# One attention and channel-mix kernel: early constants, diagonals in pieces, and another order of transposes, loads and gate products

## The chip, the cores and the metric

The kernel runs on one core of one Trainium2 chip. The metric is the device time of an execution in microseconds (us). TensorE (PE) multiplies matrices; VectorE (DVE), ScalarE (ACT) and GpSimd (POOL) work elementwise; SyncE (SP) issues DMA transfers, which 16 DMA engines carry out. Each engine runs its own instructions strictly in order, and an instruction waits at the head of its engine's queue until what it needs is there.

## The reference

Two layers, in float32. The first is a local attention over 768 positions in 24 chunks of 32: a chunk's queries see 16 keys to the left, its own 32, 8 to the right, and 8 memory keys. The second is a channel mix on the attention's output x, `[4, 768, 512]`:

```
xk = mu_k * x + (1.0 - mu_k) * x_prev        # x_prev: x one position earlier
xr = mu_r * x + (1.0 - mu_r) * x_prev
k  = np.maximum(xk @ w_k, 0.0)               # 512 -> 1024
v  = k * k @ w_v                             # 1024 -> 512
r  = 1.0 / (1.0 + np.exp(-(xr @ w_r)))       # 512 -> 512
out = r * v
```

The weights arrive as 64-bit floats, and the kernel turns each 1 MB chunk of them into two float32 parts, high and low. Every product of the channel mix is made of three matmuls (high x high, high x low, low x high).

## The kernel before, in words

The 3072 positions are worked on in 12 units of 256, each of two tiles of 128. An operation has a name of a kind and a number. For unit u: `s` scores, `max`, `sub`, `exp`, `sum`, `norm` the softmax. For tile t: `qk`, `vw` the loads of its queries and keys, and of its values; `t` the transposes of the softmax (tile pt), `bd` the two copies of these out of PSUM into `aTz`, `a` the products with the values (tile px), `x` their copy. Then, for unit u again, `mix` (for unit 0 done on PE with diagonal matrices, tile xf; for units 1 and 2 on DVE from a difference `df`), `xh`, `xl` the high and low parts of the mixed input, `g` the gate products (pr, in the last units gps and gpc), `h` the hidden products (ph), `relu`, `sq`, `kh`, `kl`, `v` the value products (pv), `sig` the sigmoid, `o` and `out`. The ten weight chunks are `w0` to `w9` (w0, w1 of w_r; w2 to w5 of w_k; w6 to w9 of w_v): `load`, `mag` on ACT, `low` and `join` on DVE, then `hi` and `lo`. Block `h0.n` of unit 0 needs chunk w(2+n), `g0.n` chunk wn, `v0.n` chunk w(6+n).

From unit 3 on the value products, from unit 6 on the hidden products, and in the last two units the gate products are made with seven block products in place of eight. The weight forms that this needs lie in DRAM and are loaded per unit (`f`, tiles wkh, wkl, wvh, wvl from `forms`).

Two things set the order on every engine. The list `FIRST` (L52) names operations one after the other, with the engine of each; they are recorded in just that order. What it doesn't name, a planner (`Plan.walk`) places by estimated costs and due times, and the due times come from the order of PE's products, `te_order`, whose lead is `LEAD` and which places the last units by rules. So a change in `FIRST` or in `te_order` also moves operations on ACT, DVE and POOL behind it, and can give an operation with a choice to another engine. Buffers of one kind (`big` for qk loads and raw weights, `vw`, `m` for PSUM banks) are handed on in turn, so a load waits on SP for the last reader of its buffer, and all loads behind it wait too.

Around the change: L393 and L394 issue the identity and mu from SP. `diagonals(m)` records for each m one operation `dg{m}` on ACT with nine instructions: (1 - mu), then four diagonals of mu and four of (1 - mu), which `mix0.m` reads. L1815 to L1819 hold back the later qk and vw loads: such a load waits for the first product whose due time lies 3 behind that of a given `a` or `s`. L1828 fills PE's idle time at the start with matmuls on zeros (tile warm) as long as no hidden product of unit 0 has been recorded.

Of the kernel before, what the change touches and what calls it, by code (L numbers as in the profile page):

```python
# [51 lines left out]
FIRST = """  # L52
qk0@dma s0@pe qk1@dma max0@dve sub0@dve exp0@act s0b@pe max0b@dve mu@dma id@dma sum0@dve norm0@pool qk3@dma qk2@dma
w2.load@dma dg1@act vw0@dma vw1@dma w3.load@dma sub0b@dve exp0b@act sum0b@dve norm0b@dve dg0@act w2.mag@act s1@pe
t0@pe w4.load@dma bd0.0@act t1@pe w2.low@dve bd0.1@dve a0@pe w2.join@dve w2.hi@dve max1@dve sub1@dve qk5@dma
w2.lo@pool bd1.0@act bd1.1@act a1@pe qk4@dma x0@act x1@act mix0.0@pe mix0.1@pe w3.low@dve w3.mag@act w3.join@dve
vw2@dma exp1@act vw3@dma sum1@dve w5.load@dma w4.low@dve norm1@dve w4.mag@act w4.join@dve xh0.0@act w3.hi@act t2@pe
xl0.0@dve s2@pe xh0.1@act w4.hi@act bd2.0@act w0.load@dma bd2.1@dve w1.load@dma t3@pe bd3.1@act bd3.0@act a2@pe x2@act
xl0.1@dve w3.lo@dve qk6@dma a3@pe max2@dve h0.0@pe w4.lo@pool w5.mag@act w5.low@dve x3@act sub2@dve w5.join@dve
h0.1@pe h0.2@pe w0.low@dve vw4@dma exp2@act w0.mag@act sum2@dve w1.low@dve w5.hi@act w5.lo@dve h0.3@pe qk7@dma  # L60
w1.mag@act w0.join@dve w0.hi@act norm2@dve t4@pe w1.join@dve t5@pe w0.lo@dve relu0.1@act df1@dve relu0.0@act sq0.0@act
vw5@dma w1.hi@act bd5.1@act bd4.0@act w1.lo@dve sq0.1@act s3@pe g0.0@pe g0.1@pe relu0.2@act w7.load@dma mix1.1@dve
w6.load@dma mix1.0@dve bd4.1@act sq0.2@act kh0.1@act bd5.0@act xh1.1@dve xl1.1@dve w7.low@dve kl0.1@dve kh0.2@act
w8.load@dma xh1.0@act a4@pe xl1.0@dve kh0.0@act relu0.3@act kl0.0@dve w8.low@dve w7.mag@act w6.mag@act w9.load@dma
w7.join@dve w6.low@dve w6.join@dve sig0.0@act sig0.1@act a5@pe g1.0@pe g1.1@pe h1.0@pe sq0.3@act kh0.3@act h1.1@pe
kl0.3@pool x4@dve w7.hi@act x5@dve max3@dve sub3@dve sig1.0@act w7.lo@pool kl0.2@dve relu1.0@act sig1.1@act w6.hi@act
df2@dve w8.mag@act sq1.0@act w9.low@dve w6.lo@dve h1.2@pe h1.3@pe relu1.2@act relu1.1@act w9.mag@act relu1.3@act
sq1.2@act v0.0@pe w8.join@dve w9.join@dve sq1.3@act w8.hi@act mix2.1@dve v0.1@pe exp3@act w9.hi@act w8.lo@dve v0.2@pe
kh1.0@dve kl1.0@dve sq1.1@act w9.lo@dve kh1.1@act kl1.1@dve xh2.1@act xl2.1@dve mix2.0@dve kh1.2@act kl1.2@pool
v0.3@pe  # L70
"""
# [228 lines left out]
def local_attention__then__channel_mix(  # L300
# [1523 lines left out]
    busy = 0.0  # L1824
    with tc.manual_schedule():
        for o in plan.order(FIRST.split()):
            if o.eng == "pe":
                n = 0 if ("ph", 0, 0) in T else int((o.start - busy - 0.1) / (0.86 if busy else 1.72))  # L1828
                for _ in range(n):
                    warm = warm or ps("mat0", "warm")  # L1830
                    nc.tensor.matmul(warm, zero, zeros, start=True, stop=True)
# [51 lines left out]
```

## Time and profile before

| | us |
|---|---|
| median of 3 runs | 390.83 (390.39 to 391.03) |
| profiled execution | 391.06 |
| its span, first to last instruction | 389.3 |

| engine | busy us | share of the span |
|---|---|---|
| PE | 380.3 | 98% |
| DVE | 336.6 | 86% |
| ACT | 274.2 | 70% |
| POOL | 16.0 | 4% |

Times in the trace count from the start of the span. The profiled execution is 1.76 us longer than its span. A busy PE is not a useful PE: the matmuls on zeros count as busy, and matmuls overlap, so that the time between two starts says more than the duration of one.

### The profile page before, as it was taken

Reading aid. Unit: us, or ns where it says so; the run is one execution under the profiler, and the core shown is the slowest. Engines: PE = TensorE matmul, PEld = TensorE weight load, DVE = VectorE, ACT = ScalarE, POOL = GpSimd, SP = SyncE. Lnnn points to the kernel's source line nnn. Section 1 sums busy time; section 2 is a strip of 40 time slices with the busy share of each in tenths; the row PEclk is TensorE's granted clock in tenths of the full one; section 3 lists DMA queues with packets and bytes.
Section 4 is the critical chain, followed back from the end, with each engine's and each line's share of the span. In section 5 each row is a group of like instructions: output and inputs, shape, how many; then the busy total and the mean of one; then the engine's idle time right before and its main releaser. Section 6 shows DMA issues by size and latency. Waiting matters only on the chain.

```text
span 389.3 us, 11106 instructions
## 1 busy us (share of the span) xinstructions
PE 380.3 (98%) x4768; PEld 352.4 (91%) x4768; DVE 336.6 (86%) x570; ACT 274.2 (70%) x468; POOL 16.0 (4%) x15
## 2 busy tenths in 40 slices
PE   7799999999999999999999999999999999999996
PEld 3589889888988999999999999999999899999996
DVE  3699999888898999969989989898999797978784
ACT  3877796914796789676578689877587857588741
POOL 2221004010000000000010000000000000000000
PEclk9999999999999999999999999999999999999999
DMA  8999870411053345435387576644056611043011
GB/s 313 414 374 368 318 309 2 141 56 54 2 197 124 130 137 199 148 127 223 117 298 226 190 272 206 209 182 145 2 163 183 199 53 56 28 136 109 0 56 54
DMA packets 25344, 63.43 MB, mean 163 GB/s; under 512 B 2512, under 2 KB 9040, under 8 KB 24784
## 3 DMA queue, kind: packets, MB, share of 16 engines
q1 hardware_dynamic: 25296, 62.73, 45.5%
q8 instruction: 37, 0.61, 0.6%
q14 instruction: 11, 0.09, 0.1%
HBM read 52.24 MB, written 10.49 MB: 161 GB/s over the span
## 4 chain that ended last, share of the span: by engine, by line
PE 91%; DMA 5%; ACT 2%; DVE 1%; SPq 0%; issue 0%
PE ph L1374 15%; PE pr L1350 14%; PE pc L1710 10%; PE pv L1350 9%; PE pa L1710 6%; PE B L1069 6%; PE pb L1710 6%; PE px L619 6%; PE G L1069 4%; PE A L1069 4%; PE s L522 4%; PE pt L602 2%; DMA vw<-in_vw_dram 2%; PE xf L673 2%; DMA wvl<-forms 1%; PE gps L1274 1%
## 5 line engine op out<-in xcount | busy, mean ns | idle before, releaser
L1374 PE MATMUL ph<-xh,wkh 128*128 128x256 f32 x192 | 53.5, 279 | 0.0
L1374 PE MATMUL ph<-xh,wkl 128*128 128x256 f32 x192 | 53.2, 277 | 0.1
L1374 PE MATMUL ph<-xl,wkh 128*128 128x256 f32 x192 | 53.1, 276 | 0.0
L1374 PEld LDWEIGHTS ph<-xh,wkl 128*128 128x128 f32 x192 | 36.1, 188 | 0.3 <-DVE wkl L450 0.3
L1374 PEld LDWEIGHTS ph<-xh,wkh 128*128 128x128 f32 x192 | 36.0, 188 | 0.3
L1374 PEld LDWEIGHTS ph<-xl,wkh 128*128 128x128 f32 x192 | 36.1, 188 | 0.0
L1657 DVE TENSOR_TENSOR khl<-k,khl 128x512 fp32r<-128x512 f32 x42 | 28.8, 688 | 6.2 <-ACT khl L377 5.7
L1350 PE MATMUL pr<-wrh,xh 128*128 128x512 f32 x80 | 31.4, 392 | 0.0
L1350 PE MATMUL pr<-wrh,xl 128*128 128x512 f32 (+1 forms) x97 | 31.3, 351 | 0.0
L1350 PE MATMUL pr<-wrl,xh 128*128 128x512 f32 x80 | 31.2, 390 | 0.0
L377 ACT CAST khl<-k 128x512 fp32r<-128x512 f32 x47 | 29.2, 621 | 2.2 <-PE pa L1710 0.9
L1350 PE MATMUL pv<-wvh,khl 128*128 128x512 f32 (+1 forms) x97 | 30.3, 390 | 0.0
L1710 PE MATMUL pa<-wvh,khl 128*128 128x256 f32 x144 | 28.2, 281 | 0.0
L1710 PE MATMUL pc<-wtbig,khl 128*128 128x256 f32 x216 | 28.2, 280 | 0.0
L377 ACT COPY aTz<-pt 64x512 f32<-64x512 f32 x43 | 24.8, 580 | 4.0 <-PE pt L602 3.6
L1710 PE MATMUL pb<-wtx,khl 128*128 128x256 f32 x216 | 27.6, 277 | 0.0
L1477 ACT ACTIVATE k<-ph 128x512 f32<-128x512 f32 x23 | 13.5, 597 | 19.1 <-PE ph L1374 17.1
L619 PEld LDWEIGHTS px<-aTz,vw 128*64 128x64 f32 x768 | 23.5, 138 | 3.5 <-DVE aTz L379 1.7
L1710 PEld LDWEIGHTS pc<-wtbig,khl 128*128 128x128 f32 x216 | 26.0, 188 | 0.1
L619 PE MATMUL px<-aTz,vw 128*64 128x64 f32 x768 | 25.5, 224 | 0.6 <-DVE aTz L379 0.6
L1710 PEld LDWEIGHTS pb<-wtx,khl 128*128 128x128 f32 x216 | 26.0, 188 | 0.0
L1710 PEld LDWEIGHTS pa<-wvh,khl 128*128 128x128 f32 x144 | 23.1, 188 | 0.3
(215 smaller groups left out, 1042.8 us busy)
## 6 DMA issues: line engine op xcount, KB each, us to landing
vw<-in_vw_dram SPq DMA_DIRECT2D x24, 512.0 KB, 5.1
ring<-in_qk_dram SPq DMA_DIRECT2D x16, 672.0 KB, 5.8
out_dram<-o SPq DMA_DIRECT2D x22, 256.0 KB, 2.1
qk<-in_qk_dram SPq DMA_DIRECT2D x8, 672.0 KB, 6.3
raw<-in_w_k_dram SPq DMA_DIRECT2D x4, 1024.0 KB, 7.5
raw<-in_w_v_dram SPq DMA_DIRECT2D x4, 1024.0 KB, 7.7
wvh<-forms SPq DMA_DIRECT2D x12, 256.0 KB, 3.4
wvl<-forms SPq DMA_DIRECT2D x12, 256.0 KB, 3.8
```

The costliest lines, as they stand in the source:

```text
L377: e.copy(dst, src)
L522: nc.tensor.matmul(room(h, c)[CHUNK * j : CHUNK * (j + 1), r, :], q4[z, r, j, :], k3[z, r, STEP * j : STEP * j + NK], start=True, stop=True,)
L602: nc.tensor.transpose(p[:, n * P : (n + 1) * P], e[:, n // 2, c, n % 2, :], id_sb)
L619: nc.tensor.matmul(p3[64 * h : 64 * h + 64, 2 * g : 2 * g + 2, CHUNK * j : CHUNK * j + CHUNK], v[:, g, h, j, :], a[:, h, g, j, :], start=True,
L673: nc.tensor.matmul(z, T["diag", m][:, j, k], x[:, k, 1 - j : 1 - j + UTOK], start=j == 0, stop=j == 1)
L1069: nc.tensor.matmul(z, w, x[:, k], start=q in (1, 7) and i + k + m == 0, stop=i + k == 2 and m == 2, skip_group_check=q not in (1, 7),)
L1274: nc.tensor.matmul(z, xs[x][:, k, c * P : (c + 1) * P], ws[w][:, k], start=q in (1, 7) and c + k + m == 0, stop=c + k == 2 and m == 2, ski ...
L1350: nc.tensor.matmul(p[:, a : a + step], x, w[:, a : a + step], start=start, stop=stop and a + step == DM)
L1374: nc.tensor.matmul(z, w, x[:, k], start=start, stop=stop)
L1477: e.activation(r, T["ph", u, f], AF.Relu)
L1657: nc.vector.tensor_sub(T["al", u, name], block(at), T["ah", u, name].bitcast(F32))
L1710: nc.tensor.matmul(p, l[:, i], r[i], start=start, stop=stop, skip_group_check=not fresh)
```

## The change

Four edits. The identity and mu are loaded from ACT's queue, as the first entries of `FIRST`. `diagonals` records three operations for each m: `mu{m}`, `dg{m}a` (four diagonals of mu), `dg{m}b` (four of 1 - mu), and `FIRST` places them apart. `FIRST` is a new list, longer than before (it now reaches into unit 2); in it, among much else, `t0` stands ahead of `s1`, `t2`, `t3`, `s2` and `a2` follow each other, `a3` and `s3` stand behind unit 0's hidden products, and the vw3 load behind qk7. In `te_order` two gate products of the last pair of units stand earlier, and the value load of tile 22 (`2 * NU - 2`) is held back to a due time 9 behind instead of 3.

```diff
 FIRST = """
-qk0@dma s0@pe qk1@dma max0@dve sub0@dve exp0@act s0b@pe max0b@dve mu@dma id@dma sum0@dve norm0@pool qk3@dma qk2@dma
+id@dma mu@dma qk0@dma mu1@act s0@pe qk1@dma mu0@act max0@dve sub0@dve dg1a@act s0b@pe dg1b@act max0b@dve sub0b@dve
+exp0@act sum0@dve qk3@dma qk2@dma norm0@dve dg0a@act t0@pe s1@pe exp0b@act sum0b@dve w2.load@dma norm0b@dve vw0@dma
...
@@ te_order
                 if u == nu - 2:
                     r = [("g", u, n) for n in range(len(GATES))]
-                    seq += h[:12] + r[:2] + v[:2] + h[12:] + r[2:5] + v[2:]
+                    seq += h[:12] + r[:2] + v[:2] + h[12:] + r[2:5] + v[2:5] + r[5:6] + v[5:]
...
             elif u == nu - 1:
-                seq += r[5:6] + v[:2] + r[6:] + v[2:]
+                seq += r[6:] + v
@@ the body of the kernel
-    o_id = op("id", ("dma", 0.2), lambda: nc.sync.dma_start(id_sb, ident))
-    o_mu = op("mu", ("dma", 0.1), lambda: nc.sync.dma_start(mu_sb[:, 0:2], mu))
+    o_id = op("id", ("dma", 0.2), lambda: nc.scalar.dma_start(id_sb, ident))
+    o_mu = op("mu", ("dma", 0.1), lambda: nc.scalar.dma_start(mu_sb[:, 0:2], mu))
@@ diagonals(m)
-        def f():
+        def f_rest():
+            nc.scalar.activation(mu_sb[:, 2 + m], mu_sb[:, m], AF.Copy, scale=-1.0, bias=1.0)
+
+        def f(j):
             T["diag", m] = k2[m].rearrange("p i t -> p (i t)").rearrange("p (j k n) -> p j k n", j=2, k=KT)
-            nc.scalar.activation(mu_sb[:, 2 + m], mu_sb[:, m], AF.Copy, scale=-1.0, bias=1.0)
-            for j in range(2):
-                for k in range(KT):
-                    nc.scalar.activation(T["diag", m][:, j, k], id_sb, AF.Copy, scale=mu_sb[:, m + 2 * j, k : k + 1])
+            for k in range(KT):
+                nc.scalar.activation(T["diag", m][:, j, k], id_sb, AF.Copy, scale=mu_sb[:, m + 2 * j, k : k + 1])
 
-        diag[m] = (op(f"dg{m}", ("act", 2.0), f, [o_id, o_mu], new=d), d)
+        o = op(f"mu{m}", ("act", 0.2), f_rest, [o_mu])
+        o = op(f"dg{m}a", ("act", 1.22), lambda: f(0), [o_id, o], new=d)
+        diag[m] = (op(f"dg{m}b", ("act", 1.22), lambda: f(1), [o], use=d), d)
@@ the late loads
-            o.deps.append(next(y for y in line if y.due > x.due + 3))
+            o.deps.append(next(y for y in line if y.due > x.due + (9 if o.name == f"vw{2 * NU - 2}" else 3)))
@@ the matmuls on zeros
-                n = 0 if ("ph", 0, 0) in T else int((o.start - busy - 0.1) / (0.86 if busy else 1.72))
+                n = 0 if ("xf", 0, 0, 0) in T or ("xf", 0, 1, 0) in T else int((o.start - busy - 0.1) / (0.86 if busy else 1.72))
```

ACT before, from its first instruction: `e` is the softmax of unit 0 in two halves (L550), `k_81` and `k_80` hold the diagonals of m = 1 and m = 0 (L407), `xx` the magnitude of w2, `aTz` the copies of the transposes.

```order
L550 ACT_TABLE_LOAD
L550 ACTIVATE e_149<-e_149 128x512
L404 ACTIVATE mu_sb<-mu_sb 128x4
L407 ACTIVATE k_81<-id_sb,mu_sb 128x128 x8
L550 ACTIVATE e_149<-e_149 128x512
L404 ACTIVATE mu_sb<-mu_sb 128x4
L407 ACTIVATE k_80<-id_sb,mu_sb 128x128 x8
L437 ACTIVATE xx<-raw_198 128x1024
L377 COPY aTz_78<-pt_300 64x16x32
```

ACT now, from the same place (lines are those of the changed kernel: L561 the softmax, L416 the diagonals, L448 the magnitude, L385 the copies).

```order
L401 DMA id_sb<-in_ident_dram 128x128
L402 DMA mu_sb<-in_mu_dram 128x8
L411 ACT_TABLE_LOAD
L411 ACTIVATE mu_sb<-mu_sb 128x4 x2
L416 ACTIVATE k_81<-id_sb,mu_sb 128x128 x8
L561 ACTIVATE e_153<-e_153 128x512
L416 ACTIVATE k_80<-id_sb,mu_sb 128x128 x4
L561 ACTIVATE e_153<-e_153 128x512
L416 ACTIVATE k_80<-id_sb,mu_sb 128x128 x4
L385 COPY aTz_78<-pt_217 64x16x32
L448 ACTIVATE xx<-raw_291 128x1024
L385 COPY aTz_79<-pt_303 64x16x32 x2
```

One set of diagonals and both (1 - mu) moved ahead of the first half of the softmax, the other set is split around its second half, and one copy of a transpose moved ahead of the magnitude.

PE before, from the matmuls on zeros ahead of unit 1's scores to the end of the mixing products (s scores, pt transposes, px products with the values, xf mixing; then pt and s of unit 1 and its px).

```order
L1831 MATMUL warm<-zero_sb 128x512
L673 MATMUL xf_366<-xTs,k_80 128x256 x4
L673 MATMUL xf_371<-xTs,k_80 128x256 x4
L673 MATMUL xf_376<-xTs,k_81 128x256 x4
L673 MATMUL xf_381<-xTs,k_81 128x256 x4
L602 MATMUL pt_408<-id_sb,e_336 128x128 x4
L522 MATMUL s_416<-qk_360 32x64 x32
L522 MATMUL s_416<-qk_338 32x64 x32
L602 MATMUL pt_491<-id_sb,e_336 128x128 x4
L619 MATMUL px_498<-aTz_78,vw_389 64x2x32 x16
L619 MATMUL px_523<-aTz_79,vw_392 64x2x32 x16
L1374 MATMUL ph_0_543<-xh_0_404,wkh_66 128x256
```

PE now, over the same stretch.

```order
L1842 MATMUL warm<-zero_sb 128x512
L684 MATMUL xf_372<-xTs,k_81 128x256 x4
L684 MATMUL xf_377<-xTs,k_81 128x256 x4
L684 MATMUL xf_384<-xTs,k_80 128x256 x4
L684 MATMUL xf_389<-xTs,k_80 128x256 x4
L613 MATMUL pt_400<-id_sb,e_333 128x128 x4
L613 MATMUL pt_415<-id_sb,e_333 128x128 x4
L533 MATMUL s_428<-qk_367 32x64 x32
L533 MATMUL s_428<-qk_365 32x64 x32
L630 MATMUL px_497<-aTz_78,vw_335 64x2x32 x16
L1385 MATMUL ph_0_528<-xh_0_408,wkh_66 128x256
```

The mixing for m = 1 comes first, the two transposes stand together ahead of the scores, and only one tile's products with the values are left ahead of the hidden products.

SP before, in the late part with the loads of weight forms for the second last pair of units (L1035) and the value loads of tiles 22 and 23 (L595).

```order
L1035 DMA wvh_87<-forms 128x2x256
L1035 DMA wvl_91<-forms 128x2x256
L595 DMA vw_4199<-in_vw_dram 128x1024
L1035 DMA wvh_86<-forms 128x2x256
L1035 DMA wvl_90<-forms 128x2x256
L1035 DMA wvh_87<-forms 128x2x256
L1035 DMA wvl_91<-forms 128x2x256
L595 DMA vw_4366<-in_vw_dram 128x1024
```

SP now, at the same place (L1046 the forms, L606 the value loads).

```order
L1046 DMA wvh_87<-forms 128x2x256
L1046 DMA wvl_91<-forms 128x2x256
L1046 DMA wvh_86<-forms 128x2x256
L1046 DMA wvl_90<-forms 128x2x256
L1046 DMA wvh_87<-forms 128x2x256
L1046 DMA wvl_91<-forms 128x2x256
L606 DMA vw_4296<-in_vw_dram 128x1024
L606 DMA vw_4366<-in_vw_dram 128x1024
```

The value load of tile 22 moved behind the last four loads of forms. Operations that change their engine in the start-up are norm0 (POOL to DVE), w2.hi, bd2.1, xh1.1, x4, x5 and kh1.0 (DVE to ACT), xh1.0, kl0.3 and w7.lo (to DVE), df1 and kl0.0 (DVE to POOL).

## Rows read from the trace of the kernel before

**Rows 1.** The page: busy time, and two of the costliest groups.

```profile
PE 380.3 (98%) x4768; PEld 352.4 (91%) x4768; DVE 336.6 (86%) x570; ACT 274.2 (70%) x468; POOL 16.0 (4%) x15
...
L377 ACT COPY aTz<-pt 64x512 f32<-64x512 f32 x43 | 24.8, 580 | 4.0 <-PE pt L602 3.6
...
L1374 PEld LDWEIGHTS ph<-xh,wkl 128*128 128x128 f32 x192 | 36.1, 188 | 0.3 <-DVE wkl L450 0.3
```

**Rows 2.** The chain of waits: start us, us, engine, tile, line, instructions.

```profile
11.30 2.33 ACT k L407 x8
13.63 1.15 ACT xx L437
...
16.00 2.08 PE px L619 x64
...
19.29 7.15 PE xf L673 x32
...
28.32 0.37 SPq L423
...
38.27 0.65 DVE raw L440
38.91 1.14 DVE wkl L450
...
42.88 0.87 PE pt L602 x8
...
52.85 5.67 PE pr L1350 x25
58.52 10.90 PE ph L1374 x96
...
91.22 5.47 PE pr L1350 x25
...
299.33 5.75 DMA wvl<-forms
```

**Rows 3.** Timeline of PE: start us, us, operation; in brackets idle time before.

```profile
29.26 2.08 PE L619 MATMUL px<-aTz,vw 128*64 128x64 f32 x64 [0.39 <-DVE aTz L379]
31.27 0.38 PE L1374 MATMUL ph<-xh,wkh 128*128 128x256 f32 x1
...
305.13 0.39 PE L1069 MATMUL B<-khl,wvl 128*128 128x256 f32 x1 [0.93 <-DMA wvl<-forms]
```

**Rows 4.** Windows: engines' busy time; last, granted clock, DMA share, GB/s.

```profile
5.00:27.00 22.00, 18.85 (x399) 13.83 (x406) 17.74 (x30) 16.20 (x36) 3.40 (x2) 1.00 1.02 412
27.00:29.00 2.00, 1.87 (x132) 1.54 (x114) 1.60 (x3) 1.52 (x4) 0.92 (x1) 1.00 0.75 213
```

**Rows 5.** DMA, issues near 7.0, 28.3, 36.1, 354.5: KB, us to landing.

```profile
vw<-in_vw_dram SPq DMA_DIRECT2D x1, 512.0 KB, 9.4
...
raw<-in_w_r_dram SPq DMA_DIRECT2D x1, 1024.0 KB, 7.8
...
qk<-in_qk_dram SPq DMA_DIRECT2D x1, 672.0 KB, 5.7
...
wvl<-forms SPq DMA_DIRECT2D x1, 256.0 KB, 3.9
```

**Rows 6.** Timeline of SP's issues: the first two value loads, and qk7.

```profile
6.16 0.99 SPq L595 DMA_DIRECT2D vw<-in_vw_dram  x2
...
36.15 0.33 SPq L483 DMA_DIRECT2D qk<-in_qk_dram  x1
```

**Rows 7.** Timeline of POOL and DVE: subtractions on POOL, mixing steps on DVE.

```profile
18.01 2.36 POOL L450 TENSOR_TENSOR wkl<-xx,wkh 128x1024 fp32r<-128x1024 f32 x1 [7.38 <-DVE wkh L379]
59.16 3.41 POOL L450 TENSOR_TENSOR wvl<-mag,wvh 128x1024 fp32r<-128x1024 f32 x1
...
46.77 3.25 DVE L787 SCALAR_TENSOR_TENSOR xx<-xx,mu_sb,xTs 128x256 f32<-128x256 f32 x8
...
78.71 2.73 DVE L787 SCALAR_TENSOR_TENSOR xx<-xx,mu_sb,xTs 128x256 f32<-128x256 f32 x4
```

More of the change, by code (lines that the diff above doesn't have):

```diff
@@ L52 @@
 FIRST = """
-qk0@dma s0@pe qk1@dma max0@dve sub0@dve exp0@act s0b@pe max0b@dve mu@dma id@dma sum0@dve norm0@pool qk3@dma qk2@dma
[L54 to L67, printed above, removed]
@@ L68 @@
-sq1.2@act v0.0@pe w8.join@dve w9.join@dve sq1.3@act w8.hi@act mix2.1@dve v0.1@pe exp3@act w9.hi@act w8.lo@dve v0.2@pe
-kh1.0@dve kl1.0@dve sq1.1@act w9.lo@dve kh1.1@act kl1.1@dve xh2.1@act xl2.1@dve mix2.0@dve kh1.2@act kl1.2@pool
-v0.3@pe
+id@dma mu@dma qk0@dma mu1@act s0@pe qk1@dma mu0@act max0@dve sub0@dve dg1a@act s0b@pe dg1b@act max0b@dve sub0b@dve
+exp0@act sum0@dve qk3@dma qk2@dma norm0@dve dg0a@act t0@pe s1@pe exp0b@act sum0b@dve w2.load@dma norm0b@dve vw0@dma
+dg0b@act bd0.1@dve max1@dve bd0.0@act t1@pe w2.low@dve a0@pe vw1@dma w2.mag@act w3.load@dma w4.load@dma sub1@dve
@@ new lines @@
+vw2@dma bd1.1@act w2.join@dve bd1.0@act a1@pe x0@act x1@act w3.low@dve exp1@act sum1@dve qk5@dma qk4@dma w3.mag@act
+w3.join@dve mix0.1@pe w4.mag@act mix0.0@pe w4.low@dve w5.load@dma w2.hi@act norm1@dve w3.hi@act t2@pe xh0.1@act
+xh0.0@act w4.join@dve w2.lo@pool bd2.0@act bd2.1@act t3@pe xl0.1@dve w0.load@dma xl0.0@dve s2@pe w5.mag@act w5.low@dve
+w3.lo@dve a2@pe w1.load@dma qk6@dma w4.hi@act bd3.1@act w5.join@dve bd3.0@act max2@dve sub2@dve w4.lo@pool h0.0@pe
+h0.1@pe w5.hi@act w1.low@dve w1.mag@act vw4@dma w0.low@dve w5.lo@dve w0.mag@act qk7@dma h0.2@pe w0.join@dve exp2@act
@@ new lines @@
+sum2@dve w0.hi@act h0.3@pe vw3@dma a3@pe w1.join@dve norm2@dve vw5@dma s3@pe w0.lo@dve x2@act relu0.0@act w8.load@dma
+w6.load@dma relu0.3@act t4@pe x3@act relu0.1@act t5@pe w1.hi@act bd5.1@act w7.load@dma df1@pool bd4.0@act w9.load@dma
+bd4.1@act sq0.0@act bd5.0@act kh0.0@act w8.mag@act sq0.1@act max3@dve w1.lo@dve mix1.1@dve mix1.0@dve w6.mag@act
+g0.0@pe w7.mag@act a4@pe xh1.0@dve vw7@dma kh0.1@act xl1.0@dve a5@pe w9.low@dve w8.low@dve g0.1@pe xh1.1@act kl0.1@dve
+relu0.2@act w6.low@dve w9.mag@act sig0.0@act w8.join@dve h1.0@pe sub3@dve kl0.0@pool w6.join@dve w8.hi@act w7.low@dve
@@ new lines @@
+sq0.3@act xl1.1@dve h1.1@pe w8.lo@dve x4@act sq0.2@act relu1.0@act vw6@dma h1.2@pe sq1.0@act w6.hi@act kh0.2@act
+relu1.1@act w6.lo@dve kl0.2@dve wz0.01@dve kh0.3@act w7.join@dve qk8@dma x5@act wz0.11@dve kl0.3@dve relu1.2@act
+sig0.1@act w7.hi@act wz0.t3@dve wz0.h3@act h1.3@pe w7.lo@dve wz0.l3@dve g1.0@pe relu1.3@act w9.join@dve v0.0@pe
+w9.hi@act df2@dve sq1.1@act wz0.00@dve sq1.2@act qk9@dma w9.lo@dve kh1.0@act v0.1@pe kh1.1@act wz0.t1@dve mix2.1@dve
+wz0.t2@dve wz0.10@dve kl1.0@dve v0.2@pe v0.3@pe exp3@act wz0.t4@dve kh1.2@act wz0.h2@act kl1.1@dve sq1.3@act kl1.2@pool
@@ new lines @@
+wz0.h1@act kh1.3@act o0.1@dve o0.0@dve sig1.0@act wz0.l1@dve mix2.0@dve kl1.3@dve wz0.h4@act wz0.l4@dve wz0.l2@dve
+sum3@dve g1.1@pe v1.0@pe xh2.1@act out0.1@dma v1.1@pe wz1.01@dve xh2.0@act xl2.0@dve wz1.11@dve wz1.t3@dve v1.2@pe
+xl2.1@dve wz1.h3@act sig1.1@act h2.0@pe wz1.l3@dve o1.0@dve wz1.00@dve h2.1@pe wz1.t1@dve wz1.10@dve wz1.t2@dve
+wz1.t4@dve wz1.h1@act wz1.l1@dve wz1.h2@act wz1.h4@act wz1.l2@dve out0.0@dma h2.2@pe v1.3@pe wz1.l4@dve wz2.01@dve
+relu2.1@act sq2.1@act wz2.11@dve wz2.t3@dve wz2.h3@act g2.0@pe relu2.2@act norm3@dve wz2.l3@dve wz2.00@dve wz2.t1@dve
@@ L71 @@
+wz2.h1@act wz2.10@dve wz2.t2@dve wz2.l1@dve relu2.0@act wz2.h2@act wz2.t4@dve o1.1@dve wz2.l2@dve out1.1@dma sq2.2@act
+wz2.h4@act g2.1@pe wz2.l4@dve sq2.0@act wz3.01@dve wz3.11@dve kh2.1@act out1.0@dma wz3.t3@dve t6@pe kh2.2@act t7@pe
+kh2.0@act kl2.1@pool kl2.0@pool kl2.2@pool sig2.0@act sig2.1@act h2.3@pe
 """
```

## The prediction

> **What bounds the kernel now.** I read the busy shares first: TensorE (PE) works for nearly all of the span, no other engine does, and a copy out of a transpose costs ACT 0.58 us, a number needed below [rows 1]. So the end can only move by what PE waits, or by what its instructions cost one by one. The chain of waits says where PE stops being what is waited for [rows 2]. Early on the chain lies on ACT: the second set of eight diagonals at 11.30, the magnitude of the first weight chunk (`w2.mag`) at 13.63, then the products with the values (`a0`, `a1`, tile px) at 16.00, two matmuls that only keep PE busy, and the mixing products (xf) at 19.29. From there PE runs almost gap-free to the end. The reader is to see that a microsecond gained before 19.29 is kept only if every later operand and load comes a microsecond sooner too.
>
> Third, the few places after 19.29 where PE still stood: 0.39 before `a2` at 29.26, for the copies of its transposes; 0.93 at 305.13, for a load of weight forms [rows 3]; and 0.3 inside the first hidden products, for the low half of a weight chunk on DVE, `w5.lo`, the last row of [rows 1]. Fourth, the DMA engines: saturated at 412 GB/s from 5 to 27 us, then 213 GB/s for two microseconds [rows 4]. In those two the loads of w0 and w1 had not been issued, since they wait for buffers that DVE and PE free. Early on, then, PE waits for ACT, and the DMA engines are close behind.
>
> **The change part by part.** *Identity and mu from ACT's queue, diagonals in four pieces.* Before, ACT made dg1 between the two halves of the softmax and dg0 behind them, 2.33 us each [rows 2]. Now both (1 - mu) and all of dg1 stand ahead of the first exponential, where ACT waited for scores, and dg0 is cut around the second exponential. 2.33 us leave ACT's queue ahead of the copies. ACT also issues two DMAs now, in the same empty time. All this costs nothing as long as the identity lands 2.5 us before the scores of the first half are ready; if not, each microsecond of lateness comes off the 2.33.
> What is late next is `a1`. Its values were issued at 6.66 (the second of the pair that begins at 6.16 [rows 6]) and landed 9.4 later [rows 5], at 16.05. On ACT, `w2.mag` (1.15) and then the two copies of t1 (0.58 each) stand behind the copy of t0. `w2.mag` began at 13.63 before; with a copy ahead of it I let it begin at 14.1, and the copies end at 16.4. So I start `a1` at 16.4 (bounds 16.1, the landing, and 17.04, as before). It takes 1.04, half of the 2.08 at 16.00; then come 1.2 from its end to the mixing products, as before (18.08 to 19.29), since the two idle matmuls are still there. Mixing starts at 18.64: **-0.65** (0 to -0.95).
> The DMA engines moved 412 GB/s in that stretch whichever queue filled them [rows 4]; another queue brings no byte of qk or vw sooner. The Trainium skill says so too ("DMA: Bandwidth & Descriptors", section "Issuing engines are not separate DMA queues"): DMAs from several engines interleave on the same 16 DMA engines, and only the time to issue is saved. By that rule the values of `a1` land where they did and hold back most of the 2.33; the trace agrees.
>
> *Order t2 t3 s2 a2, with a3 and s3 behind the first hidden products.* The copies for `a2` now run beside s2, so its 0.39 goes: **-0.4** (0 if DVE or ACT is late). `w5.lo` stands behind `w1.low` on DVE, as before. w1 was issued at 28.32 and landed 7.8 later [rows 2, 5]; w0 ahead of it is issued sooner now, since `w4.join` stands earlier on DVE. I let the wait of 0.3 go: **-0.3** (bounds -0.3 and +1.2, the latter if w1 still lands at 36.1: then two shifts of 0.65 and 1.14 for `w5.lo` [rows 2] end at 38.6, and PE wants it at 29.2 + 3 x 2.72 = 37.4).
>
> *The vw3 load moved behind qk7.* This is the price. `a3` comes right after the hidden products. These began at 31.27 [rows 3]; less 1.04 for `a3`, which stood ahead, less 0.65 and 0.4, they begin at 29.18, and with 10.90 for four blocks [rows 2] end at 40.08. The loads up to vw3 are now the same set as those up to qk7 before, and those had landed at 36.15 + 5.7 = 41.85 [rows 5, 6]. Recovered is the dip: two microseconds at 213 instead of 412 GB/s, 0.97 [rows 4]. So vw3 lands near 40.9 and PE waits: **+0.8** (0, if it lands by 40.1, to +1.8, if nothing is recovered). Queued behind `a3` are s3, t4, t5 and both gate blocks, all of PE.
>
> *g0.1 behind a5, g1.0 and g1.1 behind h1, h2 ahead of g2.* The same products in another order. Where PE goes from small-tile work (px, pt, s) to full products a block of 25 takes 5.67 instead of 5.47 [rows 2]. From mixing on there is one such passage more: **+0.2**. In exchange h1.0 now follows `a3` after 58.52 - 42.88 - 5.67 + 0.2 = 10.2 us of PE work [rows 2]. In that time x3, df1 (now on POOL), w1.lo, eight mixing steps, the cast and the subtraction must pass: 0.6 + 2.4 + 1.2 + 3.25 + 0.7 + 1.2 = 9.35 (POOL's 2.36 and DVE's 3.25 from [rows 7]; w1.lo and the subtraction as the 1.14 of [rows 2] with a hop; the cast estimated from the 0.65 of a shift over a tile of that size). It fits, barely: **+0.1** (0 to +2.5, next).
> POOL's subtraction of this size took 2.36 alone and 3.41 when DVE worked from SBUF at its side; four mixing steps that took half of 3.25 took 2.73 while POOL ran [rows 7]. The Trainium skill has a rule that speaks against putting df1 and kl0 on POOL ("GPSIMD Engine Reference", section "1. Specifications"): POOL shares its SBUF interfaces with VectorE, with contention where VectorE reads two SBUF inputs. The trace bears it out; by it my 9.35 becomes up to 9.35 + 1.05 + 2.2 = 12.6.
>
> *vw22 later.* The load of weight forms that PE waited for was issued at 299.33 and took 5.75 [rows 2], with a value load of 512 KB right behind. The same last of four loads near 354 us, with none behind, took 3.9 [rows 5]. 1.85 less is more than the 0.93 that PE stood: **-0.93** (0 if the value load is not the cause). The two loads of tiles 22 and 23 now stand behind all of that unit's forms, and have some 10 us before use.
>
> *r5 and r6 of the last gates earlier.* No small tile beside them, same products, the end of the last unit unchanged: 0. Their cover is the seven products of the last unit behind them; a sigmoid that came late would cost under 1 us at the end.
>
> **Sum.** -0.65 - 0.4 - 0.3 + 0.8 + 0.2 + 0.1 - 0.93 = -1.18. The profiled execution took 391.06 (span 389.3 and 1.76 around it) and would take 389.88; it lies 0.23 above the median of 390.83. Against the median: 389.65, so 389.7.
>
> **Rivals.**
> A, the loads govern. vw3 lands at 41.85 as qk7 did, `a3` waits 1.8, and the start-up is given back: -1.18 + 1.0 = -0.2, **390.6**. For it: full DMA engines all the way to 41 us. Against it: the dip at 27 us has a cause that the change moves.
> B, all loads in time. vw3 lands by 40.1 and df1's chain fits: -1.18 - 0.8 - 0.1 = -2.1, **388.75**. For it: w4.join and w5.join, which free buffers, are earlier on DVE. Against it: it asks for nearly twice the recovery that the dip holds.
> C, slower. df1 on POOL meets DVE's w0.lo and w1.lo, takes 3.41, and the eight mixing steps beside kl0.0 on POOL take 5.46: the chain from `a3` to h1.0 lasts 12.6 against 10.2 of PE work, so PE waits 2.4 and the sum is -1.18 + 2.3 = +1.1, **391.95**. It decides from a wait of 2.1 at h1.0 on. For it: both durations are in the trace. Against it: both at once, over the whole length, are not.
> D, the wait at 305 stays: the form load is late by itself. -1.18 + 0.93, **390.6**. Against it: the 3.9 at 354.
>
> **How the numbers follow.** Forecast 0.47, A 0.20, B 0.15, C 0.12, D 0.06. About 0.2% (0.78 us) is what a measurement of this kernel can tell from no change. The forecast's own range is 389.1 to 390.3, four fifths of it faster by that bound; with B that is 0.53, and a little of A and D brings it to 0.57. The rest of forecast, A and D is no change, 0.30; C and what I have not seen, 0.13. The range runs from below B (mixing as soon as the values allow) to above A: 388.5 to 391.2.
>
> **What would show it.** Right: mixing products at 18.4 to 18.9; no wait before `a2`; `a3` waiting for a load of vw near 40 us, by half a microsecond to one; no wait for forms near 304. Wrong: mixing at 19.2 or later (the identity lands late, or the copies wait for something else); a wait of over 1.5 at `a3` (A); a wait at h1.0 for xl or xh (C); a new wait among the second unit's value products, for weight halves that are now wanted some 3.5 us sooner. That last would upset the sum most, as I gave it no term.

## The result, and the profile after

The changed kernel is slower: 395.39 us (394.88 to 396.37, 4 runs) against 390.61 (390.07 to 391.03, 4 runs) beside it, a ratio of 1.0121 (1.0103 to 1.0139), or 4.7 us. The prediction was 389.7. The profiled span grew from 389.3 to 393.4.

The page of the changed kernel, in the groups that answer to [rows 1]: PE is as busy as before and waits more.

```profile
PE 380.5 (97%) x4766; PEld 352.5 (90%) x4766; DVE 337.9 (86%) x562; ACT 278.4 (71%) x475; POOL 18.6 (5%) x17
...
L1385 PE MATMUL ph<-xh,wkl 128*128 128x256 f32 x192 | 53.3, 278 | 1.6 <-DVE wkl L461 1.6
L1385 PE MATMUL ph<-xl,wkh 128*128 128x256 f32 x192 | 53.3, 278 | 0.9 <-DVE xl L713 0.9
```

Where PE waits is read from its timeline (start, duration, operation; in brackets idle time before, and what ended it), the stretch of [rows 3] and what follows.

```profile
20.02 7.14 PE L684 MATMUL xf<-xTs,k 128*128 128x256 f32 x32
...
29.63 1.15 PE L630 MATMUL px<-aTz,vw 128*64 128x64 f32 x32
30.71 0.38 PE L1385 MATMUL ph<-xh,wkh 128*128 128x256 f32 x1
...
39.11 0.28 PE L1385 MATMUL ph<-xl,wkh 128*128 128x256 f32 x1
40.98 0.38 PE L1385 MATMUL ph<-xh,wkl 128*128 128x256 f32 x1 [1.59 <-DVE wkl L461]
...
43.69 1.15 PE L630 MATMUL px<-aTz,vw 128*64 128x64 f32 x32
...
47.03 0.47 PE L1361 MATMUL pr<-wrh,xh 128*128 128x512 f32 x1
48.77 0.50 PE L1361 MATMUL pr<-wrl,xh 128*128 128x512 f32 x1 [1.27 <-DVE wrl L461]
...
56.48 0.39 PE L1385 MATMUL ph<-xh,wkh 128*128 128x256 f32 x1
57.74 0.38 PE L1385 MATMUL ph<-xl,wkh 128*128 128x256 f32 x1 [0.87 <-DVE xl L713]
```

Four things are to be seen. Mixing (xf) begins at 20.02, 0.73 later than the 19.29 of [rows 2]: `w2.mag` starts at 15.15 and the copies for `a1` end at 17.56, where 14.1 and 16.4 were predicted. `a2` (29.63) has no wait, and neither has `a3` (43.69). And there are three waits for DVE that the kernel before has not, or hardly (0.3 at `w5.lo`): 1.59 for `w5.lo` within the hidden products, 1.27 for `w0.lo` within the first gate product, 0.87 for the low half of unit 1's operand. What DVE and POOL did at those times (their timelines):

```profile
23.55 2.51 POOL L461 TENSOR_TENSOR wkl<-xx,wkh 128x1024 fp32r<-128x1024 f32 x1 [20.60 <-ACT wkh L385]
31.35 3.30 POOL L461 TENSOR_TENSOR wkl<-mag,wkh 128x1024 fp32r<-128x1024 f32 x1 [5.29 <-ACT wkh L385]
45.62 2.02 POOL L788 TENSOR_TENSOR xx<-xTs 128x1024 f32<-128x1024 f32 x1 [10.97 <-ACT xTs L385]
...
23.75 3.39 DVE L572 TENSOR_TENSOR e<-e,sm_sb 128x1024 f32<-128x1024 f32 x1
...
32.33 3.40 DVE L455 SCALAR_TENSOR_TENSOR mag<-mag,raw 128x1024 uint32<-128x1024 uint32 x1
...
39.70 1.22 DVE L461 TENSOR_TENSOR wkl<-mag,wkh 128x1024 fp32r<-128x1024 f32 x1
...
45.80 2.91 DVE L461 TENSOR_TENSOR wrl<-mag,wrh 128x1024 fp32r<-128x1024 f32 x1
```

An undisturbed DVE instruction of this shape takes 1.22 (39.70). `norm1` (23.75) took 3.39, `w5.join` (32.33) 3.40, `w0.lo` (45.80) 2.91, and each of them ends 1.07 or 1.08 after POOL's instruction beside it: 27.14 after 26.06, 35.73 after 34.65, 48.71 after 47.64. DVE did not go slower; it stood until POOL had finished, and then did nearly all its work. In the kernel before, POOL made `w2.lo` at 18.01 [rows 7], while DVE worked on scores in PSUM. In the changed list `w2.hi`, which it needs, is cast on ACT behind `w4.mag`, and so `w2.lo` starts 5.5 later, just ahead of `norm1`.

Marks far from the start show what was lost in which stretch. The chain of waits of the changed kernel (start, length, engine, tile), and below it that of the kernel before at the same work: the first products of the form pa, and the first of the form gps.

```profile
146.61 1.57 PE pa L1721 x12
...
307.77 2.83 PE B L1080 x24
...
358.01 2.81 PE gps L1285 x24
```

```profile
141.39 1.57 PE pa L1710 x12
...
353.96 2.81 PE gps L1274 x24
```

Up to mixing +0.73; from there to pa 126.59 instead of 122.10, +4.49; from pa to gps 211.40 instead of 212.57, -1.17 (the 0.93 before the form products [rows 3] is gone, the x24 at 307.77 runs through); the rest of the 4.1 is +0.1 behind it. The diff's last edit, which ends the matmuls on zeros at the mixing products, plays no part: neither trace has one behind 19.4.

### The profile page after: what moved, and what is told of

It reads as the page before. It is cut to its first block, busy times and chain, and to the rows that moved or that the text cites. A ratio compares the mean times of both kernels' runs of the same rounds, so it can differ in the third digit from the quotient of the medians.

```text
span 393.4 us, 11107 instructions
## 1 busy us (share of the span) xinstructions
PE 380.5 (97%) x4766; PEld 352.5 (90%) x4766; DVE 337.9 (86%) x562; ACT 278.4 (71%) x475; POOL 18.6 (5%) x17
## 4 chain that ended last, share of the span: by engine, by line
PE 85%; DVE 9%; issue 2%; DMA 1%; ACT 1%; ACTq 0%
PE ph L1385 14%; PE pr L1361 13%; PE pc L1721 10%; PE pv L1361 8%; PE pa L1721 7%; PE B L1080 6%; PE pb L1721 6%; PE px L630 5%; PE G L1080 4%; PE A L1080 4%; PE s L533 3%; PE pt L613 2%; DVE mag L455 2%; DMA mu_sb<-in_mu_dram 1%; PE gps L1285 1%
## 5 line engine op out<-in xcount | busy, mean ns | idle before, releaser
L1385 PEld LDWEIGHTS ph<-xh,wkl 128*128 128x128 f32 x192 | 36.1, 188 | 1.8 <-DVE wkl L461 1.8
L385 ACT CAST khl<-k 128x512 fp32r<-128x512 f32 x48 | 29.6, 620 | 2.6 <-PE pv L1361 1.5
L385 ACT COPY aTz<-pt 64x512 f32<-64x512 f32 x44 | 25.5, 580 | 5.5 <-PE pt L613 3.4
L1721 PE MATMUL pa<-wvh,khl 128*128 128x256 f32 x144 | 28.3, 281 | 0.0
```

The source lines that it names most:

```text
L385: e.copy(dst, src)
L1385: nc.tensor.matmul(z, w, x[:, k], start=start, stop=stop)
L1721: nc.tensor.matmul(p, l[:, i], r[i], start=start, stop=stop, skip_group_check=not fresh)
```

## The experiments

Diffs with names such as `w2.lo@pool` are of the list `FIRST`. Ratios are to the kernel before on the same chip; its median there was 391.15 (beside a_lo_dve, a_mu0, a_exp0, b_vw22), 391.21 (a_w_dve, a_lo_mu0, a_lo_idmu, b_front), 391.24 (a_pool_early, b_twice, a_w_vw3, b_best) and 390.55 (b_front_warm, b_front_mu). The planner orders what the list doesn't name anew for each kernel, so the traces are compared up to pa; in `a_lo_dve` and `a_w_dve` PE's order, by kinds of products, is the changed kernel's throughout.

### POOL's subtractions

**a_lo_dve**

```diff
-w2.lo@pool  w4.lo@pool  df1@pool  kl0.0@pool
+w2.lo@dve   w4.lo@dve   df1@dve   kl0.0@dve
```

> The changed kernel with the four subtractions that its list gives to POOL early on (w2.lo, w4.lo, df1, kl0.0) done on DVE at the same places of the list. Theory P (port): DVE operations with two SBUF inputs stood 2.2, 2.2, 1.7 and 1.0 us behind POOL; they take 7.1 less, the four subtractions add 4.0 on DVE. DVE is then 2.1 us earlier at w5.lo, so the 1.59 wait of the fourth hidden block goes, the 1.27 wait of the gate goes, and of the wait for xl 0 to 0.9 stays: 391.4 to 392.5. Rival M (mu): the late diagonals put everything 0.5 to 2 us behind and DVE is only the place where it shows; no gain over 0.5, 394.9 to 395.4.

392.06 us, ratio 1.0019 (1.0000 to 1.0039): 4.0 us of the 4.7 are gone, with mixing at 20.15, as late as in the changed kernel. As theory P said, 0.32 and 0.40 are left of the waits for DVE. Theory M falls as the main cause.

**a_w_dve**

```diff
-w2.lo@pool  w4.lo@pool
+w2.lo@dve   w4.lo@dve
```

> The changed kernel with only w2.lo and w4.lo on DVE; df1 and kl0.0 stay on POOL. Theory P: DVE's 3.39 at norm1 and 3.40 at w5.join become 1.2 each, DVE is 2.1 us earlier at w5.lo, the 1.59 wait goes to under 0.4; w0.lo still stands behind df1, so 0.5 to 1.3 of the gate's wait stays: 393.0 to 394.0. Rival: the two early collisions are not what PE waits for; 394.8 to 395.4, and df1 and kl0.0 were the whole 3.3.

392.28 us, 1.0028 (1.0014 to 1.0042), even less than expected: without the first two meetings 3.6 us of the 4.0 are gone. The third went with them, as `w0.lo` (43.56, 1.22) now starts ahead of df1 (43.75) and POOL is the one that stands, 2.78 instead of 2.02. The same DVE instructions, timeline of this kernel (`norm1`, `w5.join`, `w5.lo`):

```profile
23.59 1.22 DVE L572 TENSOR_TENSOR e<-e,sm_sb 128x1024 f32<-128x1024 f32 x1
...
31.13 1.22 DVE L455 SCALAR_TENSOR_TENSOR mag<-mag,raw 128x1024 uint32<-128x1024 uint32 x1
...
37.45 1.22 DVE L461 TENSOR_TENSOR wkl<-mag,wkh 128x1024 fp32r<-128x1024 f32 x1
```

`w5.lo` starts 2.25 earlier although DVE has two subtractions more to do, and neither the hidden products nor the gate wait.

**a_pool_early**

```diff
-w2.join@dve ... w5.load@dma w2.hi@act norm1@dve ... w4.join@dve w2.lo@pool ... w4.lo@pool
+w2.join@dve w2.hi@dve ... w2.lo@pool w3.low@dve ... w5.load@dma norm1@dve ... w4.join@dve ... w4.lo@dve
```

> The changed kernel with w2.lo still on POOL, but made early: w2.hi is cast on DVE right behind w2.join, as in the kernel before, so that POOL's subtraction runs near 19 to 21.5, beside DVE's work on PSUM; w4.lo is on DVE. Theory P: it is not POOL but the meeting with a DVE instruction of two SBUF inputs that costs; as without any early subtraction on POOL, 391.7 to 392.7. Rival: POOL's slow subtraction is the cost wherever it stands: 393.5 to 394.5.

392.33 us, 1.0025 (1.0010 to 1.0041), as P expected: the same subtraction on POOL costs nothing when it meets other work. Which work that may be, POOL and DVE show:

```profile
19.83 2.68 POOL L461 TENSOR_TENSOR wkl<-xx,wkh 128x1024 fp32r<-128x1024 f32 x1 [16.88 <-DVE wkh L387]
...
20.58 1.22 DVE L566 TENSOR_REDUCE sm_sb<-e 128x16 f32<-128x1024 f32 x1 [0.30 <-ACT e L561]
21.84 0.71 DVE L567 TENSOR_SCALAR sm_sb<-sm_sb 128x16 f32<-128x16 f32 x1
```

The reduction over 1024 elements in SBUF ran at full speed inside POOL's 2.68. The tiny `TENSOR_SCALAR` of 128x16 behind it, else 0.17, took 0.71 and ended with POOL (22.55 and 22.51).

**b_twice** (the kernel before; the second subtraction repeats the first)

```diff
         def f_lo(e):
-            e.tensor_sub(l, T["mag", i], h.bitcast(F32))
+            for _ in range(2 if i == 2 else 1):
+                e.tensor_sub(l, T["mag", i], h.bitcast(F32))
```

> The kernel before with one suspected cost doubled: POOL does its subtraction w2.lo twice in a row, the second time for nothing, from about 20.4 to 22.8, when DVE wants to join w3 (21.25, 1.23 us, two SBUF inputs). Theory P (DVE stands until POOL's instruction has ended): the join ends 1.4 later, DVE is 1.4 late at w5.lo, and PE's 0.3 at the fourth hidden block becomes 1.5 to 1.8: 392.2 to 392.8. Rival (the two share the port and each is slowed by a part): the join takes at most 1.7, 391.2 to 391.6.

392.96 us, 1.0044 (1.0028 to 1.0061), 1.7 us: P, and nothing but this one meeting was added. POOL, DVE and PE:

```profile
17.99 5.37 POOL L451 TENSOR_TENSOR wkl<-xx,wkh 128x1024 fp32r<-128x1024 f32 x2 [7.43 <-DVE wkh L379]
...
21.23 3.21 DVE L444 SCALAR_TENSOR_TENSOR xx<-xx,raw 128x1024 uint32<-128x1024 uint32 x1
...
27.80 0.66 PE L603 MATMUL pt<-id_sb,e 128*128 128x128 f32 x4 [1.38 <-DVE e L562]
```

The join ends at 24.44, 1.08 after POOL (23.36), 1.98 longer than its 1.23. I had expected the wait at `w5.lo`; it came earlier, at t2, for `norm1`.

### Early diagonals

**a_mu0**

```diff
-    o_mu = op("mu", ("dma", 0.1), lambda: nc.scalar.dma_start(mu_sb[:, 0:2], mu))
+    o_mu = op("mu", ("pool", 0.1), lambda: nc.gpsimd.memset(mu_sb[:, 0:2], 0.5))
```

> The changed kernel with mu not loaded: a memset of 0.5 on POOL stands in for it, so the output is that of another mu. The diagonals can start when the identity has landed, near 5.4. Theory M: exp0 begins at 7.7 to 7.9 instead of 9.64, mixing 1 to 1.8 us earlier, and the end follows: 393.6 to 394.4. Theory P: mixing comes earlier, but the weight halves on DVE stand behind POOL as before, and PE waits the longer for them: 394.7 to 395.4.

394.20 us (392.02 to 396.01, 6 runs), 1.0075 (1.0047 to 1.0104): inside theory M's range, and against the changed kernel's 1.0121 some 1.8 us less (0.5 to 3.1, estimated from the two intervals). Mixing came at 18.94, close to the predicted 18.64, and part of it was lost again where P said: PE waited longer for `w5.lo`, 2.29 instead of 1.59. Behind that wait the granted clock fell. Windows of the changed kernel and of this one (busy time of PE, PEld, DVE, ACT, POOL with counts; granted clock, DMA share, GB/s):

```profile
41.00:43.00 2.00, 2.00 (x17) 2.00 (x18) 2.00 (x2) 0.91 (x1) 0.00 (x0) 1.00 0.89 362
```

```profile
41.00:43.00 2.00, 1.80 (x8) 1.80 (x9) 2.00 (x3) 0.69 (x1) 0.00 (x0) 0.57 0.97 395
```

The 22 products behind the wait took 4.3 (41.20 to 45.51) instead of 2.7.

**a_exp0**

```diff
-sub0@dve dg1a@act s0b@pe dg1b@act max0b@dve sub0b@dve exp0@act
+sub0@dve s0b@pe max0b@dve sub0b@dve exp0@act dg1a@act dg1b@act
```

> The changed kernel with dg1a and dg1b put behind the first exponential instead of ahead of it. Theory M: exp0 begins at 7.6 as in the kernel before, sub0b and what follows come sooner, mixing near 19.5 (20.02 in the changed kernel): 0.3 to 0.6 less, 394.8 to 395.1. Rival: the second exponential, behind all of dg1, sets t0, and nothing is gained: 395.4.

396.24 us, 1.0129 (1.0103 to 1.0156): no gain, as the rival said. The first exponential began at 8.25, but the second waited behind all of dg1 until 12.29, and mixing came at 20.86.

**a_lo_mu0** (`a_lo_dve` and `a_mu0` together)

> Both edits at once: the four early subtractions of POOL on DVE, and a memset of 0.5 in place of the load of mu (another mu, so another output). It tells what the late mu costs once DVE is no longer held up. Theory M: mixing comes at 18.9 instead of 20.15 and the end follows, 390.6 to 391.2 against 392.06 with the subtractions alone. Rival: the next wait (the values of a0 and a1, or the weight chunks) takes it back, 391.7 to 392.2.

391.82 us, 1.0016 (1.0001 to 1.0031): the rival; of the 1.0 that mixing gained (19.16) 0.1 is in the time, give or take some 0.9 (estimated from the two intervals). One place where it went is `a3`, which now waits 0.56 for vw3.

**a_lo_idmu** (with the four subtractions on DVE)

```diff
-        "ident": np.eye(P, dtype=np.float32),
+        "ident": np.concatenate([np.eye(P, dtype=np.float32), moe_mu_k.reshape(KT, P).T, moe_mu_r.reshape(KT, P).T], axis=1),
```

> The four subtractions on DVE, and mu laid beside the identity in DRAM, so that one load of 544-byte rows from ACT's queue brings both. Theory M: what was late was the separate load of 32-byte pieces; the first diagonal starts at 5.5 to 6.0, exp0 at 8.0 to 8.4, mixing at 18.9 to 19.4, 390.8 to 391.5. Rival: any load issued there lands near 7, exp0 stays at 9.5, 392.1.

391.95 us, 1.0015 (1.0000 to 1.0030). The mechanism held, and the time hardly followed: 0.2 less than `a_lo_dve`, give or take some 0.9. ACT in the changed kernel, and below it here:

```profile
1.18 0.45 ACTq L402 DMA_DIRECT2D mu_sb<-in_mu_dram  x1
...
7.10 0.30 ACT L411 ACTIVATE mu_sb<-mu_sb 128x4 f32<-128x4 f32 x2 [4.15 <-DMA mu_sb<-in_mu_dram]
7.30 2.43 ACT L416 ACTIVATE k<-id_sb,mu_sb 128x128 f32<-128x128 f32 x8
9.64 0.61 ACT L561 ACTIVATE e<-e 128x512 f32<-128x512 f32 x1
```

```profile
5.35 0.30 ACT L410 ACTIVATE idmu<-idmu 128x4 f32<-128x4 f32 x2 [2.89 <-DMA idmu<-in_ident_dram]
5.56 2.43 ACT L415 ACTIVATE k<-idmu 128x128 f32<-128x128 f32 x8
7.93 0.63 ACT L560 ACTIVATE e<-e 128x512 f32<-128x512 f32 x1
```

mu, issued at 1.18, let ACT go on only at 7.10; laid beside the identity it came with it, at 5.35. The first exponential moved from 9.64 to 7.93 and mixing to 18.76. At pa the kernel was still 1.2 ahead of `a_lo_dve` (142.02 against 143.22), at gps only 0.4 (354.78 against 355.15). In between PE waited 0.90 for a load of forms, below, and `a_lo_dve` did not.

**b_front, b_front_warm, b_front_mu** (the kernel before with the later value loads and the early diagonals: identity and mu in one load; the same with two more idle matmuls ahead of s1; those, and two loads as in the change)

```diff
-qk0@dma s0@pe qk1@dma max0@dve sub0@dve exp0@act s0b@pe max0b@dve mu@dma id@dma ... dg1@act ... dg0@act
+id@dma qk0@dma s0@pe qk1@dma mu1@act mu0@act max0@dve sub0@dve dg1a@act dg1b@act exp0@act s0b@pe max0b@dve ... dg0a@act ... dg0b@act
```

> The kernel before with the later value loads, identity and mu in one load from ACT's queue, and the diagonals in pieces (both (1 - mu) and dg1 ahead of the first exponential, dg0 around the second); its list is otherwise unchanged, so DVE and POOL work as before. If the idea of the early diagonals is sound and only mu's landing and the order behind it spoilt it: mixing at 18.8 to 19.2, 389.3 to 390.0. Rival: the copies, the values or the weight halves take the gain back, 390.3 to 390.8 as with the later value loads alone.

> The kernel before with the later value loads and the early diagonals (identity and mu in one load), as b_front, and with one more pair of idle matmuls ahead of s1, as the kernel before has there. In b_front PE stood 1.83 within s1 and the granted clock was 0.50 from 13 to 16, so that eight transposes took 1.97 instead of 1.09 and mixing came at 20.18. If that clock is what hid the gain: clock 1.00, mixing at 18.8 to 19.2, and 390.0 to 390.4. Rival: PE still stands within s1 and the transposes end no sooner; or the gain comes at mixing and goes again at the weight halves: 390.7 to 391.2.

> The same, but identity and mu in two loads from ACT's queue, as in the changed kernel: the step as it was predicted, in the order of the kernel before. Theory M: mu lands near 7, exp0 begins at 9.5, and the first half of the softmax is 1.5 to 2 late: mixing at 19.8 to 20.3 and 391.2 to 391.8. Rival: PE's stand within s1 is what sets t0 and t1 (13.8 in the kernel before), so that up to 1.5 of lateness is free: mixing at 19.3 to 19.6, 390.6 to 391.0.

391.16, 391.25 and 390.89 us, ratios 0.9994 (0.9978 to 1.0009), 1.0000 (0.9978 to 1.0021) and 1.0007 (0.9984 to 1.0031): no change in any, and no loss either when mu is late. Both rivals of the last two hold. PE in b_front_warm, and in b_front_mu:

```profile
13.74 0.68 PE L524 MATMUL s<-qk 64*32 64x64 f32 x43 [2.34 <-issue]
14.34 1.09 PE L604 MATMUL pt<-idmu,e 128*128 128x128 f32 x8
...
20.19 7.14 PE L675 MATMUL xf<-xTs,k 128*128 128x256 f32 x32
```

```profile
13.17 0.68 PE L525 MATMUL s<-qk 64*32 64x64 f32 x43 [1.71 <-issue]
13.78 0.65 PE L605 MATMUL pt<-id_sb,e 128*128 128x128 f32 x4
...
19.39 7.14 PE L676 MATMUL xf<-xTs,k 128*128 128x256 f32 x32
```

In this order PE stands inside s1, after 85 of its 128 matmuls, for nothing that the profile shows ("issue"), in the kernel before for 1.65 until 13.21. The transposes come behind it. But the stand is not what mixing waits for throughout. b_vw22, with the start-up of before, has none in its profile (its s1 began at 11.99, behind slower matmuls on zeros, and ran through), and mixing came at 19.67, no sooner. Its chain of waits runs over the load of w2, for which `w2.mag` stands on ACT, ahead of the copies:

```profile
6.07 7.85 DMA raw<-in_w_k_dram
13.94 1.19 ACT xx L437
```

In the kernel before that load, issued at 5.79 and 7.8 on its way, landed at 13.59, just when ACT's diagonals ended (13.63 [rows 2]). So with `w2.mag` ahead of the copies, as this order has it, early diagonals had hardly anything to gain: in b_front_warm the load landed at 14.46 and mixing was late by it, although the first exponential began at 7.84, against 9.58 in b_front_mu. The changed list puts one copy ahead of `w2.mag`; no run does so in this order, so that the load and the stand were all that hid the gain is not shown. The clock in b_front was a cost of its own (windows of PE alone, b_front and then b_front_warm: 0.50, which is 1.2 GHz, and 1.00, which is 2.4) and not what hid the gain: with it at 1.00 mixing came no sooner (20.18 and 20.19).

```profile
13.00:14.50 1.50, 1.30 (x43) 0.50 1.04 423
```

```profile
13.00:14.50 1.50, 0.76 (x44) 1.00 1.06 434
```

### The value loads, and the kernel before without its waits

**b_vw22** and **a_w_vw3** (the kernel before with the edit; `a_w_dve` without it)

```diff
-            o.deps.append(next(y for y in line if y.due > x.due + 3))
+            o.deps.append(next(y for y in line if y.due > x.due + (9 if o.name == f"vw{2 * NU - 2}" else 3)))
```

> The kernel before with one edit: the two value loads of tiles 22 and 23 (8: 3 becomes 9 for the even one) are let out later. Theory: the form load that PE waited 0.93 us for was late because it shared the DMA engines with the value load right behind it; the wait goes and the kernel takes 0.9 less, 389.7. Rival: the form load is late by itself, or PE meets another load there; 390.6, no change.

> w2.lo and w4.lo on DVE, and the value loads of tiles 22 and 23 let out as early as in the kernel before (3 for both). Theory V: the value load right behind the form load is what made it late: PE's wait of some 0.9 near 305 is back, 392.8 to 393.3 against 392.28. Rival: the four form loads are late by themselves in some executions (5.7 us with no value load behind in one profile), and the edit is worth 0.4 or less: 392.2 to 392.7.

390.76 us, 0.9989 (0.9977 to 1.0001), and 392.58, 1.0035 (1.0021 to 1.0048) against 1.0028 with the edit. By both the edit brings 0.3 to 0.4, which neither tells from nothing; 0.9 stands at the edge of b_vw22's interval. The rivals fit better. In the profile of b_vw22 the wait is gone, but in a_w_vw3 there was none either, and in a_lo_idmu, where no value load is near, it is back. The chain there:

```profile
300.18 5.72 DMA wvl<-forms
305.95 1.42 PE B L1079 x10
```

The same load took 5.75 before [rows 2], 4.2 in b_vw22 and a_w_dve, and 4.5 in a_w_vw3. What makes it long in some executions stays open.

**b_best** (the kernel before with the later value loads)

```diff
-w4.hi@act bd2.0@act ... w1.low@dve w5.hi@act w5.lo@dve h0.3@pe
+bd2.0@act w4.hi@act ... w5.hi@act w5.lo@dve w1.low@dve h0.3@pe
```

> The kernel before with the later value loads and two waits taken away within its own order: bd2.0 (the copy that a2 waits for) ahead of w4.hi on ACT, and w5.lo ahead of w1.low on DVE. No work goes to POOL that wasn't there. From the rows: 0.4 for a2, 0.3 for w5.lo, 0.4 to 0.9 for the forms: 389.4 to 390.2. Rival: POOL's w4.lo, now half a microsecond later, meets w3.lo on DVE and holds back w5.lo: 390.4 to 390.8.

390.80 us, 0.9994 (0.9982 to 1.0006): nothing beyond the value loads. Both waits are gone from the profile; `a2` starts at 29.12, but the pair of px takes 2.44 instead of 2.08, as the copies for `a3` are no earlier: the wait only moved. And the rival's meeting is there, POOL and then DVE's `w3.lo`:

```profile
28.80 2.38 POOL L450 TENSOR_TENSOR wkl<-mag,wkh 128x1024 fp32r<-128x1024 f32 x1 [8.20 <-ACT wkh L377]
...
30.30 1.96 DVE L450 TENSOR_TENSOR wkl<-xx,wkh 128x1024 fp32r<-128x1024 f32 x1
```

No version beats the kernel before by more than a measurement can tell; b_vw22, at 0.9989, comes nearest.

## Why the prediction was wrong

| step | predicted | measured in the traces |
|---|---|---|
| mixing starts | -0.65 | +0.73 |
| `a2`'s wait | -0.4 | -0.39 |
| the wait for `w5.lo` | -0.3 | +1.45 |
| `a3` waits for vw3 | +0.8 | 0 |
| first gate product waits for `w0.lo` | no term | +1.40 |
| h1.0 waits for its operand | +0.1 | +1.14 |
| passages, with all that is left over | +0.2 | +0.89 |
| forms and value loads | -0.93 | -1.17 |
| last gates | 0 | +0.10 |
| sum | -1.18 | +4.15 |

The three DVE rows are differences of starts: 39.11 to 40.98 is 1.87, at the same place before 0.42; 47.03 to 48.77 is 1.74, before 0.34; 56.48 to 57.74 is 1.26, before 0.12. The +0.89 is a remainder, which no run takes apart.

*The step that failed: the wait for `w5.lo`, and with it all that I said of POOL.* I asked only whether the loads of w0 and w1 come in time, gave +1.2 as the worst, and looked for meetings of POOL and DVE only at df1 and kl0, the operations that changed to POOL. The ones that cost most had stayed on POOL: `w2.lo` and `w4.lo`, moved in time because their casts come later on ACT. a_w_dve shows that with these two on DVE 3.6 of the 4.7 us are gone. I also had w0 issued sooner; behind DVE's delay it was issued at 28.30, before at 26.94. For the gate's wait I had no term: `w0.lo` stands behind the same delay and behind df1.

*The price of a meeting.* From 2.36 against 3.41 and 2.73 [rows 7] I read that both engines get somewhat slower. The 3.41 was POOL standing until DVE let go, by this row of the kernel before, which ends at 60.30; 2.27 later, at 62.57, POOL's ends.

```profile
58.06 2.24 DVE L444 SCALAR_TENSOR_TENSOR mag<-mag,raw 128x1024 uint32<-128x1024 uint32 x1
```

b_twice and a_pool_early show what decides: whoever comes second stands until the first has ended, up to 2.2 here. The Trainium skill says it just so ("SBUF — State Buffer", section "Who interferes with whom"): an exclusive lock, in which the order of issue decides who blocks, that reductions never take, and `tensor_scalar` can. All three agree with the rows above. The page of the Trainium skill that I named in the prediction ("GPSIMD Engine Reference", section "1. Specifications") speaks of contention only, and by it I let a lock pass as a slowdown.

*Rival C* had the right mechanism and the wrong place and size. Its wait at h1.0 is there (0.87 of the 2.4 it gave), and DVE's first four mixing steps took 2.71 beside kl0.0; but most of the loss stood 17 us and more ahead of it.

*Early diagonals.* I wrote that they cost nothing as long as the identity lands 2.5 us before the scores. The condition was for the wrong load: the identity came in time, mu, a load of 4 KB issued 0.44 later, 1.7 us after it. With both in one load (a_lo_idmu) `w2.mag` started at 13.99, `a1` at 16.40 and mixing at 18.76, against the 14.1, 16.4 and 18.64 of the prediction, so the rest of the step was right. What it is worth hangs on the order around it: nothing that could be measured in the order of before, where the load of w2 lands as late as the old diagonals ended; some 1.8 in the changed kernel (a_mu0); and, once POOL's subtractions are on DVE, 0.2, which is not told from nothing (a_lo_idmu against a_lo_dve, 1.0015 and 1.0019). The gains of a_mu0 and a_lo_dve, 1.8 and 4.0, come to more than the 4.1 of both edits at once (a_lo_mu0), though the intervals are wide. How much the form loads take, I can't tell from single profiles.

*`a3` and vw3.* The wait did not come because PE was late itself; where it was early, 0.56 of the 0.8 was there (a_lo_mu0). The dip that I let vw3 recover was not filled but deeper, 86 GB/s from 27 to 29. *The forms.* The profile agreed with the term, and the timed runs gave under half of it: one row of one execution, 0.93, was taken for what every execution pays.

## What to carry to other kernels

Before moving an operation, list every POOL instruction that it moves in time, directly or through what it waits for, and look at what DVE will be doing then; a meeting costs up to the remaining length of the other's instruction, and on a full DVE most of it can reach the end (1.98 and 1.7 in b_twice). A wait that shows in one profile is worth its size only if several executions show it, and a chain that runs over one engine can hide another that ends at the same moment, as ACT's diagonals hid the load of w2. Price the small load too: what counts is the last of the loads that an instruction needs, not the largest.

## What the hardware showed unasked

- Beside a POOL subtraction in SBUF, DVE's `TENSOR_REDUCE` (1.22) and its `TENSOR_TENSOR` with an input in PSUM (1.23, at 19.30 in b_twice) were untouched, while `TENSOR_TENSOR` and `SCALAR_TENSOR_TENSOR` with two inputs in SBUF and even a `TENSOR_SCALAR` of 16 elements a partition stood until POOL's end.
- The granted clock fell to 0.57 (41 to 43 us of a_mu0, a mean over its two levels) after PE had stood 2.29, and to 0.50 (1.2 GHz) in b_front after 1.83 inside s1. It stayed at 1.00 in b_front_warm, where PE stood 2.34 there; just ahead, from 9 to 11 us, PE had been busy without a gap.
- A load of 4 KB in pieces of 32 bytes took 5.89 from issue to landing, one of 68 KB in rows of 544 bytes 4.6, from the same queue, issued at 1.18 and 0.74. Whether the pieces or the second place in the queue made it late, no run shows.
